# First mixture by folded states: state times w_in, then the softmax

## The chip, the cores and the metric

One core of a Trainium2 chip runs the whole program. The metric is the device time of one execution in microseconds. TensorE does the matrix products (the profile's PE, its weight loads PEld), VectorE is DVE, ScalarE is ACT, GpSimd is POOL; SyncE (SP) issues the transfers. TensorE's clock has two levels, 1.2 and 2.4 GHz; the profile gives the granted share of the higher one.

## The reference

```python
def _attn_ref(x, state):                    # x (4, 8, 512, 64), state (4, 8, 32, 64)
    scale = 1.0 / np.sqrt(D)
    scores = scale * np.matmul(x, state.transpose(0, 1, 3, 2))
    a = softmax(scores)                     # over the 32 states; written out with max and +1e-09
    xread = np.matmul(a, state)             # (4, 8, 512, 64)
    a2 = softmax(scale * np.matmul(state, x.transpose(0, 1, 3, 2)))   # over the 512 positions
    sread = np.matmul(a2, x)                # (4, 8, 32, 64)
    return np.concatenate([xread, sread], axis=2)

def _moe_ref(x, w_in, w_out):               # first mixture: (2176, 512) @ (512, 2048)
    h = x @ w_in
    sp = np.where(h > 20.0, h, np.log1p(np.exp(np.minimum(h, 20.0))))
    return (h * np.tanh(sp)) @ w_out        # back to 512 columns

def _moe2_ref(x, w_gate, w_val, w_out, rms_g):   # second mixture, 1536 wide
    xn = x / np.sqrt(np.mean(x * x, axis=-1, keepdims=True) + 1e-06) * rms_g
    g = xn @ w_gate
    return (g * (1.0 / (1.0 + np.exp(-g)))) * (xn @ w_val) @ w_out
```

The heads are laid side by side, so that `x` of the first mixture has 4 x 544 rows of 8 x 64 columns.

## The kernel before, in words

**Numbers.** Every large product is done in 16-bit floats at nearly 32-bit accuracy: each operand is scaled by a power of two and split into a high and a low half, and three products (high-high, high-low, low-high) are summed in PSUM. A split takes two instructions: the high half is a scaled copy (`copy_to`, lines 468 to 472, on ACT or DVE, whichever the planner picks), the low half one DVE instruction (`scalar * x - high`). The scales come from sums of squares (`norms`, `pow2`), and `prod` (line 507) multiplies them, one instruction of one column each.

**Stages.** `attention(b)` runs the softmaxes of one batch in two halves of four heads; its `reads` (line 799) is the product softmax times state in 32 bits, and lines 468/472 and 807 split the result into `slot[b]`. `group` is the first mixture for one batch (columns c = 0 to 3, 512 wide) or for all state read-outs together (c = 4, 128 wide): `l1` (line 926) multiplies by w_in, 12 products of 512 columns for each block of 128 of the 2048 hidden columns; ACT applies the activation (line 937), `gh` and `gl` (line 941) split it, `l2` (line 963) multiplies by w_out into four accumulators, and line 980 takes them out. The second mixture follows for each batch: `rms` normalises, `quad` (line 1111) is a product by a scheme of seven block products whose sums are added by DVE (line 1123), `lprod` (line 1195) the last product. `keep` loads a gate, value or output weight early, prepares it (`seven`: conversion, sums, eight splits, line 612) and writes it to memory; `load` and `load_rest` bring it back later.

**Order.** A planner (`Plan`) orders all work on each engine once, when the program is built, from costs and due times; each engine then runs its own list in that order. PSUM has four general banks (`p`) and four accumulators (`a0` to `a3`). The weight preparation for the second mixture gets a floor, an earliest due time: `KEEP0` and `KSTEP`.

The most telling place for what follows is the first addition of the second mixture (line 1123 before, line 1186 now), called **the first quad add** here. All that stands ahead of it in DVE's list must be done before it.

Of the kernel before, what the change touches and what calls it, by code (L numbers as in the profile page):

```python
# [21 lines left out]
XEXP = 15  # L22
XX, XW, XN, XK = 15, 13, 9, 22
# [295 lines left out]
def attn_moe_moe_kernel(  # L319
# [102 lines left out]
    P.fifo.update(("t", "g", "g2", "gb", "xb", "xt", "t2", "t3", "sbt"))  # L422
# [3 lines left out]
    P.pool("gb", [psm(4608 + 512 * k, 512, F16).rearrange("p (l f) -> p l f", l=2) for k in range(3)])  # L426
    P.pool("sx", [sxm(512 * k, 512) for k in range(2)])
# [49 lines left out]
    def pow2(part, pnames, k, floor, nm, xexp, most=0):  # L477
# [6 lines left out]
        t, q, s, si = small([128, n]), small([128, n], I32), small([128, n]), small([128, n])  # L484
        z = small([128, n], I32)

        def fn(e):
            if most:
                nc.vector.tensor_reduce(t, P[b][:, :k], AX.X, ALU.max)  # L489
                nc.vector.tensor_scalar(t, t, floor, 2.0 * most, ALU.max, ALU.mult)  # L490
            else:
                nc.vector.tensor_scalar(t, P[b][:, :k], floor, 2.0, ALU.max, ALU.mult)
            nc.vector.tensor_scalar(q, t.bitcast(I32), 24, None, ALU.logical_shift_right)
            nc.vector.tensor_scalar(z, q, -1, 190 + xexp, ALU.mult, ALU.add)
            nc.vector.tensor_scalar(s.bitcast(I32), z, 23, None, ALU.logical_shift_left)
            nc.vector.tensor_scalar(q, q, 64 - xexp, None, ALU.add)
            nc.vector.tensor_scalar(si.bitcast(I32), q, 23, None, ALU.logical_shift_left)

        op({"V": 0.93 + (0.13 if most else 0.0)}, fn, r=[b], w=[(nm, "s")], name=f"pow2 {nm}")
# [3 lines left out]
    def prod(nm, a, b, reads, c=1.0):  # L503

        if nm not in sc:
            t = small([128, 1])
            op({"V": 0.13}, lambda e: nc.vector.tensor_scalar(t, a, b, c, ALU.mult, ALU.mult),  # L507
               r=reads, w=[nm], name=str(nm))
            sc[nm] = t
        return sc[nm]  # L510


# [71 lines left out]
    def norms(groups, nm, xexp, who, parts=1):  # L584
# [17 lines left out]
        return pow2(part, [(nm, "n", i) for i in range(n)], n, 2.0 ** -10, nm, xexp, parts)[0]  # L602
# [29 lines left out]
    def seven(w, u, m, at, pool, after=()):  # L632
# [23 lines left out]
        for a, b in ((W11, W21), (W22, W12)):  # L656
            t = m(at + 256 + 512 * a, 512 * (b - a + 1)).rearrange("p (x y f) -> p x y f", y=2, f=256)[:, ::b - a]
            groups += [(t[:, :, :, 64 * i:64 * i + 64], qn(a, b)) for i in range(4)]
# [4 lines left out]
        for j in range(8):  # L663
            split(m, at, j, s, ((w, u), "s"), f"{w}{u}")
# [12 lines left out]
    def state_scale():  # L677
# [10 lines left out]
        s, si = pow2(part, ["xpart"], B, 2.0 ** -50, "x", XX)  # L688
# [4 lines left out]
    att_ops = []  # L693

    def attention(b, due=None):
# [17 lines left out]
        def state_t(e):  # L713
# [9 lines left out]
            e, P[sbt].rearrange("p g j n -> p (g j n)"), P[ps0]), r=[ps0], w=[sbt])  # L723
        for g in range(2):
            attention_half(b, g, xb, xbl, sbt, a_op, due)

    def attention_half(b, g, xb, xbl, sbt, a_op, due):
# [48 lines left out]
        def total(e):  # L776
            nc.vector.tensor_reduce(sm, z3(), AX.X, ALU.add)
            nc.vector.tensor_scalar(sm, sm, 1e-9, None, ALU.add)
# [11 lines left out]
        a_op({"V": 0.27}, total2, w=[e2])  # L790
        a_op({"A": a_sb(512) + 0.09, "V": v2(512) + 0.06}, lambda e: copy_to(e, P[e2], P[e2], s2), w=[e2])
        s = sc["x", b][0]
        ps2s = [bank(f"a{j}" if b < FIRST else "p") for j in range(2)]
        sls = [sl_names(b, 2 * g + j) for j in range(2)]

        def reads(e):
            for j in range(2):
                h = slice(64 * j, 64 * j + 64)
                nc.tensor.matmul(  # L799
                    P[ps2s[j]], sb[h, b, g, 2 * j:2 * j + 2, :].rearrange("p h d -> p (h d)"), P[at][h],  # L800
                    start=True, stop=True)

        a_op({"T": pe32(512)}, reads, r=[at], w=[*ps2s, *sls[0], *sls[1]], reserve=0)
        for j, (ps2, sl) in enumerate(zip(ps2s, sls)):
            a_op({"A": a_ps(512) + 0.09, "V": v1(512) + 0.06}, lambda e, j=j, ps2=ps2: copy_to(
                e, xh[:, 2 * g + j, 0, :], P[ps2], s), r=[ps2, sc["xname", b]], w=sl)
            a_op({"V": v1(512) + 0.06}, lambda e, j=j, ps2=ps2: nc.vector.scalar_tensor_tensor(
                xh[:, 2 * g + j, 1, :], P[ps2], s, xh[:, 2 * g + j, 0, :], ALU.mult, ALU.subtract),
                r=[ps2], w=sl, due=due)
# [22 lines left out]
        def twice(e):  # L832
            for r in range(2):
                copy_to(e, P[e2][:, r * D:(r + 1) * D], P[ps4][:, :D])

        a_op({"A": 0.35, "V": 0.3}, twice, r=[ps4], w=[e2])
# [40 lines left out]
    def wprod(u):  # L877
        rd = [(("wi", u), "s"), (("wo", u), "s")]
        return (prod(f"wp{u}", sc["wi", u][0], sc["wo", u][0], rd),
                prod(f"wq{u}", sc["wi", u][1], sc["wo", u][1], rd))  # L880

    def group_scale(gi, c, us):

        lo, hi = wprod(us[0])
        names = [f"wp{us[0]}", f"wq{us[0]}"]
        for n, u in enumerate(us[1:]):
            a, b = wprod(u)
            lo2, hi2 = small([128, 1]), small([128, 1])
# [608 lines left out]
```

## Time and profile before

| | |
|---|---|
| median of 3 runs | 798.05 us (796.51 to 799.89) |
| span of the profiled execution | 795.8 us |
| PE busy | 771.4 us, 97% |
| DVE busy | 649.5 us, 82% |
| ACT busy | 435.0 us, 55% |
| start of the first quad add | 415.02 us |

The span runs from the first to the last instruction; the timed median is 2.25 us above it. Busy time is the union of an engine's instructions. A mean duration is longer than the distance at which two instructions follow each other, because the next one starts before the last has ended.

### The profile page before, as it was taken

What the parts mean: (1) busy time and instruction counts of PE and PEld (TensorE: products, weight loads), DVE (VectorE), ACT (ScalarE), POOL (GpSimd) and SP (SyncE); (2) the same over time, 40 slices, a digit from 0 to 9 for tenths busy, and PEclk for the clock granted to TensorE, in tenths of its full rate; (3) what the DMA queues carried; (4) which work ended last, traced back from release to release, by engine and by line L of the source; (5) the groups of instructions that cost most, each with busy time, mean ns of one, the idle gap of its engine ahead of it and who ended that gap; (6) DMA issues with size and microseconds to landing.
All of it is one profiled execution on the core that took longest, in us unless ns stands there. A gap on an engine that the chain in (4) does not pass through costs nothing.

```text
span 795.8 us, 14238 instructions
## 1 busy us (share of the span) xinstructions
PE 771.4 (97%) x5830; PEld 528.8 (66%) x5830; DVE 649.5 (82%) x1331; ACT 435.0 (55%) x803; POOL 1.6 (0%) x7
## 2 busy tenths in 40 slices
PE   6699998999999999999999999999999999999997
PEld 4344454544444444774457588888888888999996
DVE  5989999999988798897779898986874998465661
ACT  5989999844846395776467543443340535121320
POOL 0000000000000000000000000000000000000000
PEclk9669999999999999999999999999999999999999
DMA  8571734302332543606354972439344745275001
GB/s 230 160 206 57 261 113 103 104 1 106 106 127 85 212 160 144 226 10 221 156 212 159 394 267 93 179 112 362 121 164 164 285 166 185 94 286 206 14 1 67
DMA packets 36885, 125.69 MB, mean 158 GB/s; under 512 B 20052, under 2 KB 20052, under 8 KB 30676
## 3 DMA queue, kind: packets, MB, share of 16 engines
q1 hardware_dynamic: 36820, 124.79, 44.2%
q8 instruction: 45, 0.74, 0.4%
q14 instruction: 20, 0.16, 0.1%
HBM read 101.45 MB, written 23.33 MB: 157 GB/s over the span
## 4 chain that ended last, share of the span: by engine, by line
PE 76%; DVE 13%; ACT 6%; DMA 3%; issue 1%; SPq 1%; DVEq 0%
PE p L1111 28%; PE p L926 14%; PE a L1195 14%; PE a L963 14%; PE p L1271 2%; DVE g L941 2%; DMA psm<-in_moe_w_in_dram 1%; DVE page L507 1%; DVE w2m L612 1%; DVE sxm L562 1%; PE a L1309 1%; DVE w L612 1%; PE a L799 1%; DVE w2m L578 1%; ACT junk L599 1%
## 5 line engine op out<-in xcount | busy, mean ns | idle before, releaser
L963 PE MATMUL a<-g,w2m 128*128 128x512 f16 (+1 forms) x960 | 187.2, 348 | 0.6 <-DVE slot L470 0.6
L926 PE MATMUL p<-slot,w 128*128 128x512 f16 (+1 forms) x960 | 185.9, 348 | 0.3 <-DVE page L489 0.3
L963 PEld LDWEIGHTS <-w2m 128*128 128x128 f16 x960 | 85.6, 98 | 91.0 <-issue 6.1
L926 PEld LDWEIGHTS <-w 128*128 128x128 f16 x960 | 86.3, 99 | 88.6 <-issue 2.2
L1111 PEld LDWEIGHTS <-w 128*128 128x128 f16 x1344 | 131.4, 98 | 17.6 <-issue 0.6
L1123 DVE TENSOR_TENSOR tt<-p,tt 128x512 f32<-128x512 f32 x120 | 82.2, 687 | 34.7 <-PE p L1111 33.6
L1111 PE MATMUL p<-slot,w 128*128 128x256 f16 x768 | 93.2, 273 | 0.0
L1111 PEld LDWEIGHTS <-attm 128*128 128x128 f16 x672 | 65.7, 98 | 7.8
L1195 PE MATMUL a<-attm,w2m 128*128 128x256 f16 x576 | 66.5, 273 | 0.0
L468 ACT ACTIVATE w2m<-tt 128x512 f16<-128x512 f32 x46 | 27.4, 621 | 66.0 <-DVE tt L1162 55.1
L1195 PEld LDWEIGHTS <-w2m 128*128 128x128 f16 x576 | 56.3, 98 | 7.0 <-issue 0.6
L937 ACT ACTIVATE tt<-p,page 128x512 f32<-128x512 f32 x68 | 45.8, 678 | 26.5 <-PE p L926 26.4
L1195 PE MATMUL a<-psm,g 128*128 128x256 f16 x432 | 52.1, 273 | 0.0
L941 DVE SCALAR_TENSOR_TENSOR g<-tt,page,g 128x512 f16<-128x512 f32 x68 | 50.4, 747 | 1.5 <-ACT g L468 0.6
L1147 ACT ACTIVATE tt<-tt,page 128x512 f32<-128x512 f32 x36 | 25.8, 720 | 37.8 <-DVE tt L1123 37.7
L1111 PE MATMUL p<-slot,attm 128*128 128x256 f16 x384 | 46.2, 273 | 0.0
L1195 PEld LDWEIGHTS <-g 128*128 128x128 f16 x432 | 42.3, 98 | 4.9
L468 ACT ACTIVATE psm<-psm,page 128x512 f16<-128x512 f32 (+1 forms) x36 | 25.4, 717 | 23.3 <-DVE psm L612 18.0
L1173 DVE TENSOR_TENSOR tt<-tt 128x512 f32<-128x512 f32 x48 | 32.4, 686 | 0.6
L1154 DVE TENSOR_TENSOR w2m<-tt,w2m 128x512 f16<-128x512 f32 x48 | 31.7, 684 | 0.2
L612 DVE SCALAR_TENSOR_TENSOR psm<-psm,page 128x512 f16<-128x512 f32 x40 | 29.8, 746 | 1.3 <-ACT psm L468 0.3
L567 ACT ACTIVATE sxm<-psm 128x512 uint16<-128x512 uint16 x39 | 30.0, 777 | 0.0
(202 smaller groups left out, 1077.3 us busy)
## 6 DMA issues: line engine op xcount, KB each, us to landing
w<-kept_wg SPq DMA_DIRECT2D x8, 1792.0 KB, 7.3
w<-kept_wv SPq DMA_DIRECT2D x8, 1792.0 KB, 7.3
attm<-kept_w SPq DMA_DIRECT2D x12, 1024.0 KB, 6.7
psm<-in_moe_w_out_dram SPq DMA_DIRECT2D x10, 1024.0 KB, 5.1
psm<-in_moe_w_in_dram SPq DMA_DIRECT2D x8, 1024.0 KB, 5.2
attm<-kept_wg SPq DMA_DIRECT2D x4, 1792.0 KB, 8.3
attm<-kept_wv SPq DMA_DIRECT2D x4, 1792.0 KB, 9.5
psm<-in_moe_w_gate_dram SPq DMA_DIRECT2D x6, 1024.0 KB, 5.1
```

What stands on the lines that cost most here:

```text
L468: nc.scalar.activation(o, i, ACTF.Copy, scale=1.0 if scale is None else scale)
L567: nc.scalar.activation(s16[:, :, 0], r16[:, :, 1], ACTF.Copy, scale=2.0 ** -13, bias=2.0 ** -14 - 0.5)
L612: op({"V": v1(512)}, lambda e: nc.vector.scalar_tensor_tensor(lo, f, s, h, ALU.mult, ALU.subtract), r=[*fn_, *hn, sname], w=ln, name=f"sl ...
L926: nc.tensor.matmul(P[ph][:, i * n:(i + 1) * n], part("wi", u, k, a)[:, f * 128:(f + 1) * 128], xh[:, k, b, :], start=m == 0, stop=m == 3 * ...
L937: op({"A": a_ps(512) + 0.09}, lambda e, s=s, ph=ph, ce=ce: nc.scalar.activation(P[s], P[ph], ACTF.Mish, scale=ce), r=[ph, f"ce{c}_{u}"], w ...
L941: op({"V": v1(512) + 0.06}, lambda e, s=s, g=g, u=u: nc.vector.scalar_tensor_tensor(P[g][:, 1, :], P[s], rho[u], P[g][:, 0, :], ALU.mult, ...
L963: nc.tensor.matmul(P[ya[d]][:, :n], part("wo", u, f, a)[:, d * 128:(d + 1) * 128], P[g][:, b, i * n:(i + 1) * n], start=first and m == 0, ...
L1111: nc.tensor.matmul(P[to][:, f * 256:f * 256 + 256], part(w, u, j, a)[:, k * 256 + f * 128:k * 256 + f * 128 + 128], h[:, k, b, :], start=b ...
L1123: op({"V": v1(512) + 0.06}, lambda e: nc.vector.tensor_tensor(P[to], P[bank_], P[a], ALU.add), r=[bank_, a], w=[to], name=f"{w} add")
L1154: op({"V": v1(512)}, lambda e: nc.vector.tensor_tensor(P[g][:, 1, :], P[s], P[g][:, 0, :], ALU.subtract), r=[s], w=[g], name="gl")
L1173: op({"V": v1(512)}, lambda e: nc.vector.tensor_tensor(P[o], P[a], P[b], f), r=[a, b], w=[o], name="gsum")
L1195: nc.tensor.matmul(P[to][:, t * 256:t * 256 + 256], P[g][:, a, o:o + 128], part("w2", u, j, b)[:, f * 256:f * 256 + 256], start=begin and ...
```

## The change

The reads and the first product are exchanged: (softmax x state) x w_in becomes softmax x (state x w_in).

- **Fold.** For each batch, and each quarter u of w_in's columns, `fold` multiplies the batch's states into w_in. The states of a batch stand in a block pattern, so 256 rows hold all eight heads: two banks g, each filled by six products of 64 output rows and 512 columns, in pairs j = 0, 1 that write the two halves of the partitions. The result is split (`mh`, `ml`) into one of four 512-column tiles. `l1` then multiplies by the softmax, which has 256 rows instead of 512: six products for each hidden block, not 12. The state read-outs (c = 4) keep the old way.
- **Attention.** `reads` and the splits of its result go; the softmax itself is split into two quarters of `slot[b]`, and the states are split too (128 columns, `states`). The scaling of the second softmax (`e2`) moves to the small copies behind its product.
- **Scales.** `pow2` takes three instructions in the place of five behind the first one or two; products are done for four batches or three quarters at once.
- **Second mixture's weights.** The eighth split is done not in `seven` but in `load_rest`, late, from 32 bits; `keep` writes four pieces, not one; the norms of w_out2 take two instructions, not eight. `KEEP0` goes from (100, 200) to (60, 120), `KSTEP` from 36 to 28.

```diff
@@ attention
+        stn = slotm[b].names(1024, 256)
+        for j in range(2):
+            h = slice(64 * j, 64 * j + 64)
+            a_op({"A": a_sb(128), "V": v1(128)}, lambda e, j=j, h=h: copy_to(
+                e, states(b)[:, :, j, 0, :], P[sbt][:, :, j, h], sc["x", b][0]),
+            a_op({"V": v1(128)}, lambda e, j=j, h=h: nc.vector.scalar_tensor_tensor(
+                states(b)[:, :, j, 1, :], P[sbt][:, :, j, h], sc["x", b][0], states(b)[:, :, j, 0, :],
...
@@ attention_half
-        a_op({"A": a_sb(512) + 0.09, "V": v2(512) + 0.06}, lambda e: copy_to(e, P[e2], P[e2], s2), w=[e2])
...
-        a_op({"T": pe32(512)}, reads, r=[at], w=[*ps2s, *sls[0], *sls[1]], reserve=0)
-        for j, (ps2, sl) in enumerate(zip(ps2s, sls)):
-            a_op({"A": a_ps(512) + 0.09, "V": v1(512) + 0.06}, lambda e, j=j, ps2=ps2: copy_to(
-                e, xh[:, 2 * g + j, 0, :], P[ps2], s), r=[ps2, sc["xname", b]], w=sl)
-            a_op({"V": v1(512) + 0.06}, lambda e, j=j, ps2=ps2: nc.vector.scalar_tensor_tensor(
-                xh[:, 2 * g + j, 1, :], P[ps2], s, xh[:, 2 * g + j, 0, :], ALU.mult, ALU.subtract),
+        a_op({"A": a_sb(512), "V": v2(512)}, lambda e: copy_to(e, xh[:, g, 0, :], P[at]), r=[at], w=sl)
+        a_op({"V": v1(512)}, lambda e: nc.vector.tensor_tensor(
+            xh[:, g, 1, :], P[at], xh[:, g, 0, :], ALU.subtract), r=[at], w=sl, due=due)
@@ fold, called by group
+            for a, b in ((0, 0), (0, 1), (1, 0)):
+                for j in range(2):
+                    nc.tensor.matmul(
+                        P[pm][64 * j:64 * j + 64, :], states(c)[:, g, j, a, :], part("wi", u, 2 * g + j, b),
+                        start=(a, b) == (0, 0), stop=(a, b) == (1, 0))
...
+            op({"A": a_ps(512), "V": v1(512)}, lambda e, pm=pm, m=m: copy_to(e, P[m][:, 0, :], P[pm], k),
+               r=[pm], w=[m], name="mh")
+            op({"V": v1(512)}, lambda e, pm=pm, m=m: nc.vector.scalar_tensor_tensor(
+                P[m][:, 1, :], P[pm], k, P[m][:, 0, :], ALU.mult, ALU.subtract), r=[pm], w=[m], name="ml")
@@ group, l1
+                    if c < B:
+                        for k in range(2):
+                            for a, b in ((0, 0), (0, 1), (1, 0)):
+                                f = fs[0] * 128
+                                nc.tensor.matmul(
+                                    P[ph], P[folds[u][k]][:, a, f:f + 128], xh[:, k, b, :],
+                                    start=(k, a, b) == (0, 0, 0), stop=(k, a, b) == (1, 1, 0))
+                        return
@@ seven
-        for j in range(8):
+        for j in range(7):
             split(m, at, j, s, ((w, u), "s"), f"{w}{u}")
@@ load_rest
+            f = buf(fresh("f"), "t")
+                out=P[f], in_=kept[w, u][:, 3584:]), r=[("kept", w, u, 7)], w=[f], lat=1.9, name=f"rest {w}{u}")
+            op({"A": a_sb(512) + 0.09, "V": v2(512) + 0.06}, lambda e, h=h, f=f, s=s: copy_to(e, h, P[f], s),
+            op({"V": v1(512)}, lambda e, h=h, lo=lo, f=f, s=s: nc.vector.scalar_tensor_tensor(
@@ constants
-KEEP0, KSTEP = (100, 200), 36
+KEEP0, KSTEP = (60, 120), 28
```

The planner orders everything anew. In DVE's list of before 851 of 1331 instructions stand ahead of the first quad add, now 782 of 1237. What differs among them, by kind:

| kind of DVE instruction ahead of the first quad add | before | now |
|---|---|---|
| low half of a fold (L956) | 0 | 32 |
| high half of a fold (L476, from PSUM) | 0 | 9 |
| low half of the reads (L807) | 16 | 0 |
| high half of the reads (L472, from PSUM) | 2 | 0 |
| softmax: low half (L820), high half | 0 | 9 |
| states: low half (L748), high half | 0 | 9 |
| low half of a weight split (L612, now L625) | 88 | 95 |
| scaled copies, SBUF to 16 bits (`psm`, `attm`, `w`, `w2m`) | 35 | 18 |
| products of scales (L507, now L522) | 89 | 25 |
| other instructions of a few columns | 171 | 146 |
| shift of the low words (L569, now L582) | 21 | 14 |

Conversions (68 joins and 68 signs), the 36 weight sums, the 64 `gl`, the 16 outputs of `l2` and the 70 instructions of the softmaxes are as many as before. Over the whole program the low halves of weight splits are 104 before and 95 now in `split`, with nine in `load_rest`. On PE, of the second layer's products (line 963, now 1036), 18 groups of six stand behind the first product of the second mixture before, and 21 now.

On DVE, in batch 1's attention (slot_77 is its slot, page tiles hold scales, g, attm, w and w2m are tiles of the kernel), before:

```order
L807 SCALAR_TENSOR_TENSOR slot_77<-a_87,page_68,slot_77 128x512
L784 STREAM_TRANSPOSE tt<-attm 128x512
L507 TENSOR_SCALAR page_102<-page_100,page_68 128x1
L807 SCALAR_TENSOR_TENSOR slot_77<-a_88,page_68,slot_77 128x512
L612 SCALAR_TENSOR_TENSOR w2m<-w2m,page_101 128x512
L507 TENSOR_SCALAR page_102<-page_100,page_101 128x1 x2
L507 TENSOR_SCALAR page_102<-page_68,page_101 128x1
```

Now, on DVE at the corresponding place (rms is the memory of the fold's tiles):

```order
L956 SCALAR_TENSOR_TENSOR rms<-p_86,rms 128x512
L575 TENSOR_SCALAR sxm<-psm 128x512
L591 SCALAR_TENSOR_TENSOR w2m<-w2m,sxm 128x512 x2
L809 TENSOR_TENSOR attm<-attm,page_101 128x512
L956 SCALAR_TENSOR_TENSOR rms<-p_84,rms 128x512
L522 TENSOR_SCALAR page_103<-page_68 128x4
L809 TENSOR_TENSOR attm<-attm,page_102 128x512
L811 STREAM_TRANSPOSE tt<-attm 128x512 x2
```

The low halves of the reads have gone, the low halves of folds have come, and a product of scales covers four batches.

On DVE, up to the first quad add (line 1123), before:

```order
L470 CAST xem<-rms 128x2x256
L1064 TENSOR_TENSOR xem<-rms,xem 128x2x256
L661 TENSOR_TENSOR attm<-attm 128x512
L1003 TENSOR_TENSOR rms<-rms 128x512 x2
L1123 TENSOR_TENSOR tt<-p_84,tt 128x512
L1003 TENSOR_TENSOR rms<-rms 128x512
L489 TENSOR_REDUCE page_114<-p_83 128x1
```

Now, up to the first quad add (line 1186):

```order
L625 SCALAR_TENSOR_TENSOR attm<-attm,page_68 128x512
L1154 TENSOR_SCALAR page_117<-page_117 128x1
L1151 TENSOR_REDUCE page_117<-page_117 128x1
L1152 TENSOR_SCALAR page_117<-page_117 128x1
L476 TENSOR_SCALAR g<-tt,page_117 128x512
L1014 SCALAR_TENSOR_TENSOR g<-tt,page_117,g 128x512 x2
L474 COPY tt<-p_86 128x512
L476 TENSOR_SCALAR g<-tt,page_117 128x512
L1014 SCALAR_TENSOR_TENSOR g<-tt,page_117,g 128x512 x2
L1186 TENSOR_TENSOR tt<-p_83,tt 128x512 x2
```

Before, weight sums (line 661) and 16 low halves of weight splits still stand around and behind it; now the last of the 95 weight splits (line 625) stands ahead of it.

## Rows read from the trace of the kernel before

**Rows 1.** The page: busy time by engine; the chain that ended last, by engine

```profile
PE 771.4 (97%) x5830; PEld 528.8 (66%) x5830; DVE 649.5 (82%) x1331; ACT 435.0 (55%) x803; POOL 1.6 (0%) x7
PE 76%; DVE 13%; ACT 6%; DMA 3%; issue 1%; SPq 1%; DVEq 0%
```

**Rows 2.** Windows: length, busy us of PE, PEld, DVE, ACT, POOL; clock, DMA

```profile
0.00:20.00 20.00, 13.23 (x78) 9.12 (x79) 10.73 (x25) 11.55 (x22) 1.60 (x7) 0.96 0.85 230
20.00:220.00 200.00, 187.43 (x1084) 90.72 (x1084) 189.13 (x509) 163.54 (x303) 0.00 (x0) 0.93 0.38 121
220.00:415.00 195.00, 195.00 (x1208) 101.92 (x1207) 164.02 (x319) 121.78 (x258) 0.00 (x0) 1.00 0.42 158
415.00:796.00 381.00, 375.78 (x3466) 327.03 (x3464) 285.57 (x481) 138.08 (x221) 0.00 (x0) 1.00 0.47 173
620.00:660.00 40.00, 40.00 (x369) 35.86 (x367) 39.02 (x67) 21.36 (x37) 0.00 (x0) 1.00 0.64 232
```

**Rows 3.** Timelines at the second mixture's start, PE then DVE: start, length

```profile
410.01 1.47 PE L1111 MATMUL p<-slot,w 128*128 128x256 f16 x12
415.02 0.68 DVE L1123 TENSOR_TENSOR tt<-p,tt 128x512 f32<-128x512 f32 x1
```

**Rows 4.** Waits of DVE by cause (total, times, longest): 0 to 20 us

```profile
DVE tt L470 <- PE p L739: 7.2, 2, 5.6
...
DVE attm L1411 <- issue: 0.2, 1, 0.2
```

**Rows 5.** The same from 20 to 220 us, first and last of eight

```profile
DVE attm L761 <- PE p L752: 1.4, 2, 1.3
...
DVE w2m L612 <- ACT w2m L468: 0.2, 1, 0.2
```

**Rows 6.** The same from 220 to 415 us, four of nine

```profile
DVE attm L472 <- DMA kept_w<-attm: 6.4, 1, 6.4
...
DVE psm L472 <- DMA kept_wg<-psm: 3.8, 1, 3.8
DVE attm L472 <- DMA kept_wv<-attm: 2.6, 1, 2.6
...
DVE page L489 <- PE p L481: 0.6, 1, 0.6
```

**Rows 7.** The chain that ended last: start, length

```profile
8.21 5.44 DMA psm<-in_moe_w_in_dram
...
221.21 2.59 PE p L926 x12
```

**Rows 8.** Timeline of PE around the reads (L799), 32-bit

```profile
230.21 1.99 PE L799 MATMUL p<-tt,attm 64*128 64x512 f32 x8
232.13 1.04 PE L963 MATMUL a<-g,w2m 128*128 128x512 f16 x4
```

**Rows 9.** PE: a pair of 64-row products (L752), and one whole product (L1008), 32-bit

```profile
65.06 1.08 PE L752 MATMUL p<-tt,attm 128*64 128x512 f32 x4
66.07 1.25 PE L963 MATMUL a<-g,w2m 128*128 128x512 f16 x5
...
450.64 1.02 PE L1008 MATMUL p<-rms,ones 128*128 128x512 f32 x2
451.50 1.46 PE L963 MATMUL a<-g,w2m 128*128 128x512 f16 x6
```

**Rows 10.** Timeline of DVE, 34 to 37 us

```profile
34.36 0.69 DVE L771 TENSOR_TENSOR attm<-attm,page 128x512 f32<-128x512 f32 x1
34.97 0.78 DVE L562 TENSOR_SCALAR sxm<-psm 128x512 uint16<-128x512 uint16 x2
35.64 0.74 DVE L612 SCALAR_TENSOR_TENSOR w<-w,page 128x512 f16<-128x512 f32 x1
36.30 0.74 DVE L807 SCALAR_TENSOR_TENSOR slot<-a,page,slot 128x512 f16<-128x512 f32 x1
36.96 0.68 DVE L777 TENSOR_REDUCE page<-attm 128x16 f32<-128x512 f32 x1
```

**Rows 11.** Timeline of DVE, 58 to 60 us

```profile
58.73 0.46 DVE L507 TENSOR_SCALAR page<-page,page 128x1 f32<-128x1 f32 x3
59.22 0.21 DVE L507 TENSOR_SCALAR page<-page 128x1 f32<-128x1 f32 x1
59.35 0.68 DVE L470 COPY attm<-a 128x512 f32<-128x512 f32 x1
59.95 0.48 DVE L472 TENSOR_SCALAR w2m<-w2m,page 128x512 f16<-128x512 f32 x1
```

**Rows 12.** Windows: 20 to 60 us

```profile
20.00:60.00 40.00, 31.59 (x169) 16.82 (x169) 36.27 (x91) 37.21 (x73) 0.00 (x0) 0.68 0.62 181
```

More of the change, by code (lines that the diff above doesn't have):

```diff
@@ L475, in attn_moe_moe_kernel, with pow2 @@
     sc = {}
-    def pow2(part, pnames, k, floor, nm, xexp, most=0):
+    def pow2(part, pnames, k, floor, nm, xexp, most=0, to=None):
         b = bank()
@@ L601, in norms @@
             op({"A": a_sb(size) + 0.17}, fn, r=ns, w=[q, (nm, "n", i)], name=f"sq {who}")
-        return pow2(part, [(nm, "n", i) for i in range(n)], n, 2.0 ** -10, nm, xexp, parts)[0]
+        return pow2(part, [(nm, "n", i) for i in range(n)], n, 2.0 ** -10, nm, xexp, parts, column(*nm))[0]
     def split(m, at, j, s, sname, who):
@@ L693, in attn_moe_moe_kernel, with states @@
     att_ops = []
+    def states(b):
+        return slotm[b](1024, 256, F16).rearrange("p (g j l n) -> p g j l n", g=2, j=2, l=2)
     def attention(b, due=None):
@@ L904, in group, with bounds, both @@
-    def group(gi, c, us, before, after):
+    def bounds(us):
+        for u in us:
+            scalar(("pr", u), [128, 2], lambda t, u=u: nc.vector.tensor_tensor(
+                t, pair["wi"][:, :, u], pair["wo"][:, :, u], ALU.mult), [(("wi", u), "s"), (("wo", u), "s")])
+        lo, hi, names = sc["pr", us[0]][:, 0:1], sc["pr", us[0]][:, 1:2], [("pr", us[0])]
+        for n, u in enumerate(us[1:]):
+            def both(t, lo=lo, hi=hi, u=u):
+                nc.vector.tensor_tensor(t[:, 0:1], lo, sc["pr", u][:, 0:1], ALU.min)
+                nc.vector.tensor_tensor(t[:, 1:2], hi, sc["pr", u][:, 1:2], ALU.max)
+            k = ("lohi", tuple(us[:n + 2]))
+            t = scalar(k, [128, 2], both, [*names, ("pr", u)])
+            lo, hi, names = t[:, 0:1], t[:, 1:2], [k]
+        return lo, hi, names
@@ L912, in group @@
         ya = [buf(("ya", gi, d), f"a{d}") for d in range(KD)]
-        xr = [nm for k in range(KD) for nm in sl_names(c, k)]
+        xr = [nm for k in range(KD if c == B else 2) for nm in sl_names(c, k)]
+        folds = {}
         for pi, pair in enumerate(pairs):
             gs = []
+            if c < B:
+                at = us.index(pair[0][0])
+                for u in us[at:at + 2]:
+                    if u not in folds:
+                        folds[u] = fold(c, u, pool, opened_)
             for u, fs in pair:
```

217 lines of the change are left out of this document (122 added, 95 removed).

## The prediction

> **What bounds the kernel now.** I read the page first. PE is busy 97% of the span and holds 76% of the chain that ended last [rows 1]: a kernel bound by TensorE, it seems, and the change takes work from TensorE. But such a share is a mean over stages, so the windows come next, cut where the second mixture begins. The reader is to see that DVE is no less full than PE at first: from 20 to 220 us DVE is busy 189.13 of 200 and PE 187.43; from 220 to 415 PE is full and DVE has 164.02 of 195; behind 415 PE has 375.78 of 381 and DVE 285.57 [rows 2]. So taking work from PE opens the way only as far as DVE lets it.
>
> How far is that? The timeline gives the place to ask: PE starts the second mixture at 410.01, DVE its first quad add at 415.02 [rows 3]. Each engine runs its list in order, so all of DVE's work ahead of that addition is a floor under its time, however fast PE is. The waits of DVE by cause say how much of the 415.0 us was no work: 9.0 us before 20 (six rows), 5.1 from 20 to 220 (eight rows), 24.6 from 220 to 415 (nine rows) [rows 4 to 6], together 38.7. DVE's work ahead of the first quad add, with the gaps between dependent instructions, is thus 415.0 - 38.7 = 376.3 us.
>
> **PE's terms.** The first layer's products follow each other at 2.59 / 12 = 0.216 us [rows 7]. Half of 768 go: 384 x 0.216 = -82.9. The reads go: two halves take 232.13 - 230.21 = 1.92 us, eight halves 7.7 [rows 8]. The folds add 32 x 6 = 192 products of 64 output rows, which no row shows in 16 bits. Bounds: each as long as a whole one (41.5), or a pair in the time of one (20.7). The nearest row is a 32-bit pair of such products: it holds PE from 65.06 to 66.07, 1.01 us, where a single whole 32-bit product holds it 0.86 (450.64 to 451.50) [rows 9]; so a pair costs little more than one, and I take 20.7. Sum: -69.9 us.
>
> The Trainium skill (TensorEngine Tiling, "Restrictions and Gotchas") says that column tiling does without the fast weight load. By it the folds' weights would load more slowly; were all of that in the open, the folds would cost up to the 41.5 of the upper bound. The pair above, of which each half has its own weight load, does not show such a loss. Either way the sum below does not move, since PE will not be the engine waited for.
>
> With -69.9, PE could begin the second mixture at 340 us. DVE decides whether it may.
>
> **DVE's terms, ahead of the first quad add.** Counts are from the table of the order, times are distances between starts. A low half (scalar times tensor minus tensor) takes 35.64 to 36.30 = 0.66, a tensor-tensor operation 0.61, a shift 0.67 / 2 = 0.34 [rows 10]; a product of scales 0.49 / 3 = 0.16, a scaled copy 0.48 [rows 11].
> - Fold results: 32 low and 9 high halves, 41 x 0.66 = +27.1. From PSUM such a split is not dearer: the low half of the reads, from PSUM, takes 0.66 too [rows 10].
> - Reads: 18 x 0.66 = -11.9. Softmax in their place: 9 x 0.61 = +5.5.
> - States: 9 instructions of 128 elements; between a scale's 0.16 and a shift's 0.34, I take the middle, +2.3.
> - Weight splits: 7 more low halves ahead of the mark, +4.6, though there are fewer in all: the preparation now gets earlier due times. 17 scaled copies less (ACT takes them), -8.2; 7 shifts less, -2.4.
> - Scales: 64 products and 25 other small ones less, 89 x 0.16 = -14.2.
> - What is left of the difference in count, 4 instructions of half a microsecond: -2.
>
> Sum: +0.8 us. What the change saves on scales and reads, the fold's splits cost. DVE's work ahead of the mark is 377.1 us, as before, and it now stands 37 us above PE's 340.
>
> **The waits that stay.** The 9.0 us at the start were waits for the first transposes. SP's queue now begins with w_in, ahead of x, and DVE's list with its conversion; a load of it takes 5.44 us [rows 7], so DVE starts about as late: 9.0 stays. Behind it DVE is the fullest engine throughout, as it was from 20 to 220; at that stretch's rate of 5.1 us in 200, 366 us take 9.3. The waits from 220 to 415 fell where DVE ran ahead of PE; 12.8 of them were for the write-outs of prepared weights [rows 6]. Now each write goes in four pieces, and its region comes free in parts; I leave them out of the sum and keep them for the upper bound. First quad add: 377.1 + 9.0 + 9.3 = 395.4, between 386 (no wait behind the start) and 416 (all 38.7 as before).
>
> **Behind it.** From the first quad add to the end the kernel took 795.8 - 415.0 = 380.8 us with PE full. Now 21 groups of the second layer are left behind the first product instead of 18: 3 x 6 x 0.216 = +3.9. `load_rest` adds nine splits there, 9 x (0.66 + 0.48) = 10.3 us on DVE and ACT. DVE is busy 75% in this stage and covers them, but not from 620 to 660, where it has 39.02 of 40 [rows 2] and where seven of the nine may fall, 8.0 at most in the open. I take 1. The preparation that ran there no longer does, so 0 is the other end.
>
> **Edits at nothing.** ACT: up to 415 it is busy 11.55 + 163.54 + 121.78 = 297 us [rows 2]. It gets 23 high halves of folds, most copies that DVE gives up and four table loads, some 30 us, and loses the scaling of e2 and some of the norms: about 325 in 395, covered by DVE's 377; if it were late, DVE's `gl` would be. The earlier floors move the preparation, not its amount. The four writes instead of one and the nine loads through the `t` buffers are SP's, on whose queue the next weight load stands; transfers take 42% of the DMA engines' time from 220 to 415 [rows 2].
>
> **Sum.** 395.4 + 380.8 + 3.9 + 1 = 781.1 for the span; the timed median stands 2.25 above the span, so 783 us, 1.9% less.
>
> **The rivals.**
> - *The whole of PE's saving arrives:* 798.05 - 69.9 = 728. For it speaks PE's 97%. Against it, DVE would have to do 377 us of work by 345. It would need the planner to have put much work behind the mark, and the order shows the opposite. 2 in 100. A smaller relative: DVE's waits almost vanish because PE and ACT have room; 386 at the first quad add gives 774, and a start without its 9 us 765. 12 in 100.
> - *DVE's waits come back in full:* a fold's bank is freed by DVE (`ml`), a first-layer bank was freed by ACT alone; with four general banks a late DVE holds up PE, whose next result DVE then waits for. With the 24.6 and 5.1 of before, the first quad add is at 416 and the time 803, and 794 with half of the difference. The write-outs push the same way. 14 in 100 for 794 and above.
> - *TensorE's clock falls,* the slower side. PE now has about 326 us of work (395.7 busy up to 415, less 69.9) to do in 395, with gaps between. From 20 to 60 us, where PE waited most, the granted clock was 0.68 of the higher level, against 1.00 from 220 on [rows 2, 12]. At a mean of 0.965 as before, PE's work is some 315 us at full clock. It fits into 395 while the mean stays above 0.80; below, PE decides again: at 0.75 it needs 420, the first quad add comes at 420, and the time is 808. Against it: the work comes in dense groups, and from 20 to 220 the mean was 0.93 in spite of that start. 6 in 100. The Trainium skill (TensorE: Matmul & The Clock Gate, "The HAM clock gate") says that half rate is TensorE's default and that sustained activity releases it. Rows 12 agree, with their 0.68 where PE was busy 31.59 of 40; by that rule, thinner work on PE is a danger, and only the trace of the new kernel can show how large.
>
> **How the numbers follow.** The forecast, 775 to 794 around 783, gets 66 in 100. The range 768 to 801 leaves out the whole saving, the last part of the small waits, the clock and the full return of the waits. Within 0.5% of 798.05 means 794 to 802, about what a measurement of this kernel can tell from no change. Faster: 66 + 12 + 2 = 80 in 100; the same 13; slower 7.
>
> **What would show it.** Right: the first quad add (L1186) at 395, 386 to 405; DVE busy at 94% or more from 20 us to there, with PE visibly idle for it; DVE's busy total near 649 again; PE's down by some 70; six fold products in about 0.65 us, not 1.29; from the first quad add to the end 384 to 388 us. Wrong: a first quad add before 380 (DVE's work was over-counted) or after 410 (waits on ACT, PE's banks or the write-outs); a clock well under 0.9 between 60 and 390; PE idle by more than 8 us behind the first quad add, where the late splits would be the cause.

## The result, and the profile after

The changed kernel takes 808.15 us (median of 4 runs, 806.44 to 810.53), the kernel before beside it 797.94 (796.51 to 799.89): ratio 1.0125, 95% interval 1.0098 to 1.0151. It is slower, by 1.25%, and 25 us above the forecast of 783. The profiled execution, the longest of the four, has a span of 808.7 us. Its page, busy time and the chain by engine (the answer to [rows 1]):

```profile
PE 725.2 (90%) x5606; PEld 505.7 (63%) x5606; DVE 645.5 (80%) x1237; ACT 451.6 (56%) x804; POOL 1.6 (0%) x7
...
PE 42%; DVE 14%; ACT 1%; DMA 1%; issue 1%; DVEq 0%; SPq 0%; ACTq 0%
```

PE lost 46 us of busy time, DVE 4. No engine is as full as PE was. The chain can be followed back to 324 us only, so its shares add up to 59% and are not to be set beside those of before. The windows, in the stretches of [rows 2] with the boundary at the new first quad add, then five shorter ones:

```profile
20.00:220.00 200.00, 166.14 (x1027) 82.53 (x1028) 182.38 (x420) 162.02 (x299) 0.00 (x0) 0.87 0.38 119
220.00:411.00 191.00, 166.66 (x1053) 86.88 (x1051) 167.59 (x332) 148.26 (x277) 0.00 (x0) 0.91 0.58 209
411.00:809.00 398.00, 383.58 (x3484) 329.89 (x3482) 282.68 (x455) 126.85 (x203) 0.00 (x0) 0.99 0.39 142
620.00:660.00 40.00, 35.42 (x301) 30.28 (x300) 31.99 (x59) 9.86 (x17) 0.00 (x0) 0.91 0.45 165
...
20.00:60.00 40.00, 20.53 (x142) 14.13 (x144) 38.47 (x98) 38.31 (x74) 0.00 (x0) 0.59 0.84 252
140.00:180.00 40.00, 40.00 (x191) 18.54 (x191) 27.33 (x57) 22.00 (x44) 0.00 (x0) 1.00 0.09 27
340.00:366.00 26.00, 17.10 (x219) 15.19 (x219) 24.34 (x44) 15.37 (x26) 0.00 (x0) 0.76 0.77 279
366.00:406.00 40.00, 40.00 (x184) 17.23 (x183) 28.39 (x55) 25.06 (x40) 0.00 (x0) 0.93 0.45 168
616.00:632.00 16.00, 8.84 (x56) 6.34 (x55) 10.95 (x27) 3.63 (x8) 0.00 (x0) 0.79 0.49 204
```

From 220 to 411 PE is busy for 87% and DVE for 88%: neither is full. The short windows show that the two take turns: from 140 to 180 PE is full and DVE idles for 13 us, from 340 to 366 DVE is full and PE idles for a third, from 366 to 406 PE is full and DVE idles for 12 us. Behind 411, PE has 14 us of idle time (before: 5 [rows 2]), half of it in the 16 us from 616. Timelines of the same places as [rows 3]:

```profile
406.48 1.47 PE L1174 MATMUL p<-slot,w 128*128 128x256 f16 x12
...
410.78 0.68 DVE L1186 TENSOR_TENSOR tt<-p,tt 128x512 f32<-128x512 f32 x1
```

The first quad add (the mark, in what follows) came at 410.8, not at 395.4 (before: 415.0), and from there to the end it took 808.7 - 410.8 = 397.9 us, not 385.7 (before: 380.8). So two stages lost time against the forecast: 15.4 and 12.2 us.

**Ahead of the first quad add.** The waits by cause (total, times, longest), PE's from 20 us on, then DVE's two largest:

```profile
PE p L485 <- ACT junk L612: 11.9, 5, 6.3
PE a L1036 <- DVE g L1014: 9.1, 2, 8.3
PE p L485 <- DMA attm<-in_x_dram: 7.3, 1, 7.3
...
DVE g L476 <- PE a L1036: 9.5, 3, 5.1
DVE tt L474 <- PE p L1174: 8.9, 1, 8.9
```

PE's named waits ahead of the mark are 69.2 us from the start on (before 19.3), DVE's 39.6: 6.6 to 20 us, 13.0 to 220 and 20.0 behind. Before, DVE's were 9.0, 5.1 and 25.9, together 40.0: the list from 220 to 415 us has 13 rows, of which the prediction counts nine, 24.6 us. The chain that ended last, around 365 us (start, length), shows how the lists follow each other:

```profile
360.98 0.67 DVE rms L1128 x2
...
363.04 0.61 DVE psm L476
...
363.67 0.69 DVE psm L956
...
364.96 0.61 DVE psm L956
...
365.62 8.20 PE p L988 x24
373.82 1.42 PE p L944 x12
375.23 1.40 PE p L988 x6
376.63 3.88 PE a L1036 x18
...
404.06 1.29 PE p L988 x6
```

Up to 365.6 the chain runs through DVE, from 324 on nearly without a break and mostly through the preparation of weights; behind that it is PE alone for 41 us, and this is batch 3's group. Its first folds stand at 358.69, in one block of 24 products. Of the four tiles that take its fold results (pool `m3`), three lie in `psm`, where the weights are prepared, so `fold` waits for `spare`, and `spare` for all weight conversions. `spare` issues no instruction: it is a step of the planner, and sets the folds' place in the lists.

**Behind it.** PE's waits from 411 us on, then DVE at one of the late splits of `load_rest`:

```profile
PE p L1174 <- ACT tt L472: 3.6, 2, 2.9
PE p L1174 <- DMA attm<-kept_wg: 2.6, 1, 2.6
PE p L1174 <- DVE tt L1186: 1.4, 1, 1.4
...
621.22 0.49 DVE L476 TENSOR_SCALAR slot<-tt,page 128x512 f16<-128x512 f32 x1 [3.59 <-DMA out_dram<-slot]
```

The split writes into slot 1, whose result is still being written out; ACT has the same wait (6.1 us in two). Such waits, and any named wait of PE here, are absent from the trace before.

### The profile page after: what moved, and what is told of

Its sections match the earlier page's. It is cut to its first block, busy times and chain, and to the rows that moved or that the text cites. A ratio compares the mean times of both kernels' runs of the same rounds, so it can differ in the third digit from the quotient of the medians.

```text
span 808.7 us, 13823 instructions
## 1 busy us (share of the span) xinstructions
PE 725.2 (90%) x5606; PEld 505.7 (63%) x5606; DVE 645.5 (80%) x1237; ACT 451.6 (56%) x804; POOL 1.6 (0%) x7
## 4 chain that ended last, share of the span: by engine, by line
PE 42%; DVE 14%; ACT 1%; DMA 1%; issue 1%; DVEq 0%; SPq 0%; ACTq 0%
PE p L1174 21%; PE a L1258 10%; PE a L1036 5%; PE p L988 3%; PE p L1334 2%; DVE tt L1186 2%; DVE tt L1236 1%; DMA out_dram<-slot 1%; PE a L1372 1%; DVE slot L1101 1%; DVE tt L1225 1%; DVE w2m L1217 1%; DVE rms L1128 1%; DVE attm L625 1%; DVE psm L625 1%
## 5 line engine op out<-in xcount | busy, mean ns | idle before, releaser
L1036 PE MATMUL a<-g,w2m 128*128 128x512 f16 (+1 forms) x960 | 191.9, 356 | 9.3 <-DVE g L1014 9.1
L1036 PEld LDWEIGHTS <-w2m 128*128 128x128 f16 x960 | 88.6, 102 | 99.7 <-issue 17.9
L1174 PEld LDWEIGHTS <-w 128*128 128x128 f16 x1344 | 132.0, 98 | 25.4 <-issue 7.6
L1174 PEld LDWEIGHTS <-attm 128*128 128x128 f16 x672 | 66.0, 98 | 12.8 <-DMA attm<-kept_wg 2.8
L988 PE MATMUL p<-slot,rms 128*128 128x512 f16 x288 | 70.6, 389 | 3.3 <-ACT tt L1010 3.0
L1258 PEld LDWEIGHTS <-w2m 128*128 128x128 f16 x576 | 56.3, 98 | 6.5
L988 PEld LDWEIGHTS <-rms 128*128 128x128 f16 x288 | 28.3, 100 | 40.7 <-issue 10.7
L1010 ACT ACTIVATE tt<-p,page 128x512 f32<-128x512 f32 x68 | 45.2, 678 | 14.9 <-PE p L988 13.1
L472 ACT ACTIVATE w2m<-tt 128x512 f16<-128x512 f32 x43 | 25.7, 621 | 41.5 <-DVE tt L1225 30.0
L1210 ACT ACTIVATE tt<-tt,page 128x512 f32<-128x512 f32 x36 | 25.9, 721 | 38.3 <-DVE tt L1186 38.1
L472 ACT ACTIVATE g<-tt 128x512 f16<-128x512 f32 x24 | 14.1, 621 | 51.1 <-DVE tt L1236 42.9
L472 ACT ACTIVATE g<-tt,page 128x512 f16<-128x512 f32 x39 | 27.1, 712 | 26.5 <-PE a L1036 26.5
L472 ACT ACTIVATE psm<-psm,page 128x512 f16<-128x512 f32 (+1 forms) x42 | 29.8, 715 | 9.3 <-DVE psm L625 7.3
L944 PE MATMUL p<-w,slot 128*64 128x512 f16 x192 | 26.9, 401 | 7.9 <-ACT tt L1010 4.4
```

Source lines behind the costliest of these rows:

```text
L472: nc.scalar.activation(o, i, ACTF.Copy, scale=1.0 if scale is None else scale)
L944: nc.tensor.matmul(P[pm][64 * j:64 * j + 64, :], states(c)[:, g, j, a, :], part("wi", u, 2 * g + j, b), start=(a, b) == (0, 0), stop=(a, b ...
L988: nc.tensor.matmul(P[ph], P[folds[u][k]][:, a, f:f + 128], xh[:, k, b, :], start=(k, a, b) == (0, 0, 0), stop=(k, a, b) == (1, 1, 0))
L1010: op({"A": a_ps(512) + 0.09}, lambda e, s=s, ph=ph, ce=ce: nc.scalar.activation(P[s], P[ph], ACTF.Mish, scale=ce), r=[ph, cen], w=[s], tab ...
L1036: nc.tensor.matmul(P[ya[d]][:, :n], part("wo", u, f, a)[:, d * 128:(d + 1) * 128], P[g][:, b, i * n:(i + 1) * n], start=first and m == 0, ...
L1174: nc.tensor.matmul(P[to][:, f * 256:f * 256 + 256], part(w, u, j, a)[:, k * 256 + f * 128:k * 256 + f * 128 + 128], h[:, k, b, :], start=b ...
```

## The experiments

Theory A: the late splits cost what was lost behind the first quad add. Theory B: the wait of batch 3's fold tiles makes DVE and PE take turns, and that cost what was lost ahead of it. "Ahead" sums DVE's named waits up to the first quad add; "rest" is the mark less these waits, so DVE's work there, with the short gaps between its instructions; a blank was not summed.

| kernel | us | first quad add | ahead | rest | from there to the end |
|---|---|---|---|---|---|
| before | 797.9 | 415.0 | 40.0 | 375.0 | 380.8 |
| changed | 808.2 | 410.8 | 39.6 | 371.2 | 397.9 |
| e1_split_early | 802.1 | 415.0 | 41.6 | 373.4 | 385.8 |
| e2_own_fold_tiles | 776.9 | 381.5 | 25.2 | 356.3 | 393.4 |
| e6_tiles_that_wait | 809.0 | 411.7 | 39.7 | 372.0 | 396.3 |
| e4_early_and_tiles | 763.9 | 382.9 | 24.4 | 358.5 | 378.2 |
| e13_tiles_split_later | 770.3 | 380.0 | | | 388.9 |
| e12_best_group6_tiles | 770.7 | 383.6 | | | 385.3 |
| e3_old_floors | 817.2 | 416.9 | | | 398.4 |
| e9_best_old_floors | 788.7 | 405.2 | | | 380.4 |
| e5_before_late_split | 818.3 | 432.9 | | | 384.6 |

**The eighth split early again** (e1_split_early).

```diff
@@ seven
-        for j in range(7):
+        for j in range(8):
@@ keep
-        op({"D": 0.74}, lambda e: nc.sync.dma_start(out=t[:, 3584:], in_=region(3840, 512)),
+        op({"D": 0.74}, lambda e: nc.sync.dma_start(out=t[:, 3584:], in_=region(3584, 512)),
@@ load_rest: no buffer, no split
-                out=P[f], in_=kept[w, u][:, 3584:]), r=[("kept", w, u, 7)], w=[f], lat=1.9, name=f"rest {w}{u}")
+                out=m(at, 512), in_=kept[w, u][:, 3584:]), r=[("kept", w, u, 7)], w=m.names(at, 512),
```

> The changed kernel with the eighth split of each weight done early again, in `seven`, and brought back ready by `load_rest`, as in the kernel before. Theory A (the late splits stand in DVE's list ahead of other work and wait there until slot 1 has been written out; PE waits for that work between 600 and 640 us and its clock falls): 10 to 17 us less than the changed kernel, 791 to 798, nearly all behind the first quad add; from that addition to the end 380 to 388 us instead of 397.9; no wait of DVE or ACT for the write-out of a slot, named waits of PE behind the addition under 3 us instead of 9.0. Rival (the second half is longer because more second-layer products and weight work stand in it): within 4 us of the changed kernel, 804 to 812.

802.1 us, 6.1 less. The stage behind the mark is 12.1 us shorter, the waits for a write-out are gone, and of PE's 9.0 us of named waits 0.6 are left, as theory A has it. The total is not, since the mark went up by 4.2: DVE has 2 us more work ahead of it, and PE now stands for 26.9 us at one small product for the scale of a weight (line 485), whose squares ACT had not finished:

```profile
368.75 0.58 PE L485 MATMUL p<-page,ones 128*128 128x2 f32 x2 [26.87 <-ACT junk L612]
```

**Own tiles for batch 3's folds** (e2_own_fold_tiles).

```diff
+    extra = Mem("extra", 4)
@@ pool "m3"
-                  for m, at in ((psm, 4608), (psm, 5120), (psm, 5632), (slotm[3], 1280))])
+                  for m, at in ((extra, 0), (extra, 512), (slotm[3], 1280))])
@@ order of the stages
-        spare = op(..., w=[*slotm[3].names(1280, 512), *psm.names(4608, 1536)], after=[conv], name="spare")
+        spare = op(..., w=slotm[3].names(1280, 512), name="spare")
-        opened.append(op(..., w=psm.names(4608, 1792), after=[conv, *m_users["m3"]], name="open"))
+        opened.append(op(..., w=psm.names(4608, 1792), after=[conv], name="open"))
```

> The changed kernel with three tiles of their own for batch 3's folds (two in spare memory, one in its slot) that do not wait until all weight preparation is done. Theory B (memory: batch 3's folds and first layer come only after the last weight preparation, so DVE has nothing while PE runs them, and PE had nothing before): batch 3's folds start well before 358 us, the first quad add comes at 395 to 403 instead of 410.8, and the time is 793 to 801. Rival (the order on PE follows the due times, and memory is not what holds the folds): the folds start after 345 us again, the first quad add within 4 us of 410.8, and the time 804 to 812.

776.9 us, 31.3 less than the changed kernel; ratio to the kernel before 0.9739 (0.9725 to 0.9754). It gains more than theory B expected. PE and DVE ahead of the mark, in the window, in the timelines and, last, what writes the two tiles in spare memory:

```profile
340.00:366.00 26.00, 24.18 (x119) 10.22 (x118) 24.12 (x46) 23.00 (x41) 0.00 (x0) 1.00 0.77 276
...
238.78 1.49 PE L945 MATMUL p<-w,slot 128*64 128x512 f16 x12 [1.38 <-ACT tt L1011]
...
329.76 2.11 PE L989 MATMUL p<-slot,extra 128*128 128x512 f16 x9
...
337.16 1.49 PE L945 MATMUL p<-w,slot 128*64 128x512 f16 x12
...
351.93 1.49 PE L945 MATMUL p<-w,slot 128*64 128x512 f16 x12
...
365.11 0.84 PE L945 MATMUL p<-w,slot 128*64 128x512 f16 x6
...
376.58 1.47 PE L1175 MATMUL p<-slot,w 128*128 128x256 f16 x12 [0.19 <-ACT tt L1011]
381.48 0.68 DVE L1187 TENSOR_TENSOR tt<-p,tt 128x512 f32<-128x512 f32 x1
...
L473 ACT ACTIVATE extra<-p x6: 581/592/597, 239.2 to 368.2; 128x512 f16<-128x512 f32 x6
```

Batch 3's folds and first layer now stand beside the weight preparation instead of behind it: from 340 to 366 both engines are busy for 24 of 26 us, and the clock is 1.00 there instead of 0.76. The mark comes 29.3 us earlier: 14.4 are DVE's waits, 14.9 its work; 13 of the 95 weight splits now stand behind the mark, which is 13 x 0.66 = 8.6 us of that work. Three of batch 3's eight fold results are written as early as 239 us, some 120 us before its first fold in the changed kernel, into the three tiles; the other five follow from 337 to 365 as tiles come free. Of DVE's waits, those behind 220 us fall from 20.0 to 6.7, those from 20 to 220 hardly (13.0 to 11.6).

The Trainium skill (Perfetto Trace Analysis, "Optimization Strategy") says that a kernel whose most-contended engine changes over time may gain from interleaving these regimes. This trace agrees: with the folds moved in beside the weight preparation the time is 31.3 us shorter.

**The same tiles, with the wait** (e6_tiles_that_wait).

```diff
-        spare = op(..., w=slotm[3].names(1280, 512), name="spare")
+        spare = op(..., w=slotm[3].names(1280, 512), after=[conv], name="spare")
```

> The same tiles as in e2_own_fold_tiles, but their users wait, as in the changed kernel, until all weight conversions are done; nothing else differs. Theory B (the wait costs, not the place of the tiles): batch 3's folds start after 345 us, the first quad add comes at 405 to 417, time 800 to 814. Rival (the place of the tiles or the new order as such gave the 31 us): within 5 us of e2_own_fold_tiles, 772 to 782.

809.0 us: the whole gain is gone, and waits and work ahead of the mark are those of the changed kernel again, with 95 weight splits ahead of the mark. The row at its folds, and the next wait of PE:

```profile
351.67 2.13 PE L945 MATMUL p<-w,slot 128*64 128x512 f16 x18
364.35 0.59 PE L486 MATMUL p<-page,ones 128*128 128x2 f32 x2 [10.54 <-ACT junk L613]
```

Since only the wait differs from the kernel above, with the order that the planner makes of it, theory B is shown. Here the wait is that for the conversions alone, without the memory that is the reason for it in the changed kernel.

**Both together** (e4_early_and_tiles). The edit is that of e1_split_early and that of e2_own_fold_tiles.

> Both undone together: the eighth split early again (as in e1_split_early) and three own tiles for batch 3's folds (as in e2_own_fold_tiles). If the two losses lie in different stages and add up: first quad add at 380 to 386 us, 384 to 388 us from there to the end, time 767 to 775. Rival (the nine splits that go back ahead of the mark push it up, as they did by 4 us in e1_split_early, where one PE product waited 26.9 us for the squares of a weight): first quad add at 388 or later, time 775 to 785.

763.9 us, 34 less than the kernel before, ratio 0.9567 (0.9553 to 0.9582): the best version. Its page, and its only named wait of PE behind 370 us:

```profile
PE 708.4 (93%) x5606; PEld 496.7 (65%) x5606; DVE 632.0 (83%) x1212; ACT 459.2 (60%) x827; POOL 1.6 (0%) x7
...
PE p L1175 <- ACT tt L1211: 0.6, 1, 0.6
```

The two losses lie in different stages and more than add up (6.1 + 31.3 = 37.4, together 44.3). Against e2_own_fold_tiles the mark goes up by 1.4 us, where it went up by 4.2 in e1_split_early: the longest wait of PE for a weight's squares is 3.5 us, not 26.9. And the stage behind the mark is 15.2 us shorter, not 12.1; why it gains more stays open.

**The late splits behind the write-out** (e13_tiles_split_later). Beside own tiles the late splits cost 776.9 - 763.9 = 13.0 us. Here they stay, and the first eight are called for one step later:

```diff
@@ gated, the tiles as in e2_own_fold_tiles
-                    if c + 1 >= B - 1:
-                        load_rest(c - B + 2)
+                    if c + 1 == B:
+                        load_rest(1)
...
                     for v in range(U2):
                         load("w2", v, 1)
+                    if c + 2 == B:
+                        load_rest(0)
```

> e2_own_fold_tiles (late splits kept) with the first eight of the nine late splits called for one step later, after slot 1 has been written out and well before they are needed in batch 3. Theory A (the splits wait for the write-out and hold up what stands behind them in the lists of DVE and ACT): no wait of DVE or ACT for a slot's write-out, named waits of PE behind the first quad add under 2 us instead of 7.4, and from that addition to the end 378 to 385 us instead of 393.4, the time about 762 to 770. Rival (the work of the splits in a full stretch costs, wherever they stand): 390 to 396 us from the first quad add to the end, time 773 to 780.

770.3 us: 6.6 of the 13.0 are back. The stage behind the mark took 388.9 us, between the two expectations: 4.5 of the 15.2 us between 393.4 and 378.2. One wait of 2.0 us for a write-out is left (in e2_own_fold_tiles 12.8 on DVE and ACT), and 4.3 us of PE's waits (there 7.1):

```profile
PE p L1175 <- ACT tt L1211: 1.5, 2, 0.9
PE p L1175 <- DVE tt L1187: 1.2, 3, 0.5
...
ACT slot L473 <- DMA out_dram<-slot: 2.0, 1, 2.0
```

So moving the splits away from the write-out, with the new order that this brings, takes back half of the time and less than a third of the loss behind the mark. What the rest is, the splits' own 10 us of work or the order around them, stays open.

**The late split alone, in the kernel before** (e5_before_late_split).

```diff
@@ seven
-        for j in range(8):
+        for j in range(7):
@@ keep
-        op({"D": 5.9}, lambda e: nc.sync.dma_start(out=t[:, :], in_=region(0, 4096)),
+        op({"D": 5.2}, lambda e: nc.sync.dma_start(out=t[:, :3584], in_=region(0, 3584)),
...
+        op({"D": 0.74}, lambda e: nc.sync.dma_start(out=t[:, 3584:], in_=region(3840, 512)),
@@ load_rest: as in the changed kernel
```

> The kernel before with only the late eighth split added (seven splits in `seven`, the last 512 columns kept in 32 bits, split in `load_rest`). Theory A: the span from the first quad add to the end grows by 10 to 17 us, waits of DVE or ACT for the write-out of a slot appear between 590 and 640 us, and the time is 806 to 815. Rival: DVE covers the nine splits; within 4 us of the kernel before, 794 to 802.

818.3 us, 20.3 more. The late split does harm without the folds too, but only partly as expected: PE idles for 7.3 us from 620 to 660, and for 10 from 420 to 500, where gate weights come back late (`attm<-kept_wg`, 4.9 us in one wait). PE's first quad product came at 407.5, but the add only at 432.9, since DVE had more weight preparation ahead of it; so the stage behind the mark, at 384.6, does not show the loss. The harm is shown, theory A's mechanism only for a part of it.

**The floors** (e3_old_floors and e9_best_old_floors). One line, `KEEP0, KSTEP = (100, 200), 36`, in the changed kernel and in the best one.

> The changed kernel with the earliest due times of the weight preparation as before (KEEP0 100 and 200, KSTEP 36). Rival to theory B (the earlier floors push weight preparation ahead of the first mixture's own work on DVE and ACT, and PE starves from 20 to 140 us): PE's first layer starts 10 us or more earlier, the first quad add comes before 403, time 790 to 800. Theory B: DVE's work is the same, some of it only changes places; first quad add within 5 us of 410.8, time 803 to 813.

> e4_early_and_tiles with the floors of the kernel before (KEEP0 100 and 200, KSTEP 36). If the floors matter only through the wait that e4 no longer has: within 4 us of it, 760 to 768. If the earlier floors bring something by themselves, as e3_old_floors against the changed kernel (9 us) suggests: 769 to 777, with DVE emptier before 180 us and a later first quad add.

817.2 and 788.7 us: 9.0 and 24.8 more. All expected times were missed. In the best kernel PE reaches the second mixture at 352.2 us with the old floors, but DVE still has 19 low halves of weight splits (line 626) ahead of the first quad add, at 405.2. The earlier floors are a gain.

**One engine's work doubled, in the same order** (e7, e8, e10 and e11). The low half of each fold twice (21.1 us of DVE), or the first layer's products twice (83 us of PE, the second time with the sum begun anew), in the changed kernel and in the best one:

```diff
-            op({"V": v1(512)}, lambda e, pm=pm, m=m: nc.vector.scalar_tensor_tensor(
-                P[m][:, 1, :], P[pm], k, P[m][:, 0, :], ALU.mult, ALU.subtract), r=[pm], w=[m], name="ml")
+            op({"V": v1(512)}, lambda e, pm=pm, m=m: [nc.vector.scalar_tensor_tensor(
+                P[m][:, 1, :], P[pm], k, P[m][:, 0, :], ALU.mult, ALU.subtract) for _ in range(2)], r=[pm], w=[m], name="ml")
@@ or, in l1
-                        for k in range(2):
+                        for k in (0, 1, 0, 1):
```

> The changed kernel in the same order, with the low half of each fold computed twice: 32 more DVE instructions of 0.66 us, 21.1 us of DVE work, 8 of them behind 340 us where DVE has room. If DVE's work alone sets the first quad add, as the prediction's sum has it: 16 to 21 us more than the changed kernel, 824 to 830. If DVE and PE take turns: those 14 or so that fall where PE waits for DVE (60 to 100 and 220 to 365 us) count, 8 to 14 us more, 816 to 822. If DVE's waits of 40.6 us absorb it: within 4 us.

> The changed kernel in the same order, with the six first-layer products of each hidden block computed twice, 384 more products of 0.216 us, 83 us of PE work: the number of products is that of the kernel before again. If PE's saving is hidden behind DVE's work, as the prediction's sum has it, and PE has 76 us of idle time ahead of the mark: 0 to 15 us more than the changed kernel. If DVE and PE take turns, the products in the stretches where PE is full (163 from 100 to 220 us, 96 behind 365) count in full, 35 + 21 us: 45 to 65 us more, 853 to 873. If PE decides everywhere: 75 to 83 more.

> e4_early_and_tiles in the same order, with the low half of each fold computed twice, 21.1 us more of DVE work. The prediction's step that DVE's work is the floor under the first quad add, once the wait for memory is gone: 16 to 21 us more, 780 to 785. If PE decides there too: 0 to 8 more, 764 to 772.

> e4_early_and_tiles in the same order, with the first layer's six products computed twice, 83 us more of PE work. If DVE is the floor and PE has room beside it: at most the idle time of PE ahead of the mark, some 49 of the 83 us, is absorbed, so 34 to 60 more, 798 to 824. If PE is full wherever the first layer stands (from 100 us on it is busy 39 of 40): 65 to 83 more, 829 to 847.

DVE twice: 824.0 (+15.9) and 781.7 (+17.8). PE twice: 871.2 (+63.1) and 834.1 (+70.2). In a fixed order three quarters and more of the work added here to either engine reach the end. PE's idle time ahead of the mark took up no more than a quarter of the 83 us. In the best kernel the 17.8 lie in the range for DVE as the floor, and the 70.2 in that for PE full wherever the first layer stands: both engines set the time. In the changed kernel the 15.9 fall just short of the range for DVE alone, and the 63.1 lie in that for engines that take turns.

**Group 6 on the own tiles too** (e12_best_group6_tiles).

```diff
-        group(6, 2, every, None, 2)
+        spare = op(..., w=slotm[3].names(1280, 512), name="spare")
+        group(6, 2, every, None, 2, "m3", [spare])
```

> e4_early_and_tiles with the three own tiles used by batch 2's last group too, so that the normalisation of batch 0, whose memory the other fold tiles share, need not wait for that group. If that memory still holds it up: first quad add 3 to 8 us earlier, 756 to 761. If DVE's work ahead of the mark is the floor: within 3 us, 761 to 767. Three tiles instead of four for eight quarters of folds may cost PE waits for a free tile: then 768 or more.

770.7 us, 6.8 more: the mark did not move, and the stage behind it took 7.1 us longer. So nothing shows that the normalisation's memory held the mark up; the run had one tile less for that group too, and why the stage behind the mark grew stays open.

## Why the prediction was wrong

Measured against the forecast's span of 781.1 the three parts are: DVE's work ahead of the mark 371.2 instead of 377.1 (-5.9), its waits 39.6 instead of 18.3 (+21.3), the rest of the program 397.9 instead of 385.7 (+12.2); together 27.6, the whole miss in the span of this execution.

- **DVE's work: right.** Fold splits cost what reads and scales saved; DVE's total is 645.5 us where 649 was forecast. The base was 1.3 us too high, since four rows of waits were left out of the 38.7: the work before was 375.0, not 376.3. The scaled copy's 0.48 is a length, not a distance between starts as the other prices are, which for 17 copies is half a microsecond.
- **PE's terms: right.** Twelve fold products take 181.30 - 179.88 = 1.42 us, 0.71 for six (forecast 0.65). PE's busy time fell by 46, not 70, though the products are those counted: the clock was 0.87 from 20 to 220 us and 0.91 from there to the mark (before 0.93 and 1.00 [rows 2]), and work at a lower clock takes longer (six fold products 0.84 us at 36.57, with a clock of 1.00, and 1.26 at 40.08, with 0.63). In the best kernel, with 0.94 from 20 us to the mark, busy time is 63 below that of before.
- **The waits: the step that failed.** "Behind it DVE is the fullest engine throughout [...] at that stretch's rate of 5.1 us in 200, 366 us take 9.3": they took 33.0, and DVE is busy for 350 of the 391 us from 20 to the mark, 89% where 94 was the sign of being right. The rate was carried over from a kernel in which PE was busy for 382 of the 395 us behind 20 [rows 2]. Most of the new fold tiles of batch 3 lie in the memory of the weight preparation and come free with its last conversion. The line of `spare` shows this, and the prediction gave it no price. e6_tiles_that_wait against e2_own_fold_tiles puts it at 32.1 us. At the mark it is 30.2: 14.5 are waits, and 15.7 work that now stands ahead of it; 13 of the weight splits (95, not 82) are 8.6 of that. The waits from 20 to 220 are another matter: 13.0 us instead of 5.1, of which 11.4 are for second-layer products (line 1036) while PE is full from 140 to 180; with own tiles they are there too (11.6 in e2_own_fold_tiles, 13.2 in the best kernel).
- **DVE as the only floor: wrong.** The premise that PE "will not be the engine waited for" falls with e11_best_first_layer_twice: even without the wait, 70 of 83 us of PE's work reach the end. As one of two floors it holds: e10_best_low_half_twice.
- **`load_rest`: mis-sized.** Taken at 1 us, at most 8; e1_split_early gives 12.1. The sum priced the splits' work but not the buffer they write to. With the splits early the stage takes 385.8, which fits the 3.9 for three more groups (380.8 + 3.9 = 384.7). The best kernel's 378.2 with as many groups fits it only if one counts from PE's first quad product, which does not wait for the mark: 390.2 us there (from 370.9) and 390.0 in e1_split_early (from 410.7), against 795.8 - 410.0 = 385.8 before [rows 3].
- **Floors at nothing: wrong, on the other side.** They save 9.0 us in the changed kernel and 24.8 in the best one.
- **The rivals.** The nearest was the one of waits that come back in full (794 to 803): the size was right ahead of the mark (its own sum gives 804), but the mechanism that the runs show is a wait for memory in SBUF; what PSUM banks add was not tested. The clock fell as that rival feared (0.59 from 20 to 60 us), but its mean from 20 to 411, (200 x 0.87 + 191 x 0.91) / 391 = 0.89, stayed above its 0.80. What the lower clock costs here no run separates.

Without the wait for memory and the late split, the rest of the change (the folds, the scales and the floors) gains 34 us; with them it loses 10.

## What to carry to other kernels

When a change takes work from one engine and gives it to another, look first for the buffers that the new work needs, who holds them, and until when: a wait for memory can put two engines one behind the other, as here for 32 us, and no sum of one engine's work shows it. Waits counted in the old trace hold for the new kernel only where both engines still have work beside each other. Work moved to a late stage is to be priced with the transfer that still reads its target, not by its duration alone: nine splits of 10 us cost 6.1 us in the changed kernel and 13.0 beside own tiles.

## What the runs showed of the hardware

Two products of 64 output rows run beside each other: a pair takes 2 x 1.42 / 12 = 0.237 us, one whole product 0.216 [rows 7]. PE in the changed kernel, where the clock was 1.00, and the fold's weight loads (ns, shortest, median and longest):

```profile
179.88 1.49 PE L944 MATMUL p<-w,slot 128*64 128x512 f16 x12
181.30 1.10 PE L837 MATMUL p<-attm 128*32 128x64 f32 x64
...
L944 PEld LDWEIGHTS <-slot x192: 106/110/177, 36.6 to 386.5; 128*64 128x64 f16 x192
```

The Trainium skill (TensorEngine Tiling, "Restrictions and Gotchas") says that column tiling excludes the fast weight load. The trace fits that: a load of 64 columns takes 110 ns, one of 128 columns for the first layer (line 988) 98, both medians. If this costs anything in this pattern, it is within the 10% between 0.237 and 0.216.
